# Second attention's scores made by rows in 32-wide column tiles, its maximum subtracted from PSUM, and slot products in column tiles

## The chip, the cores and the metric

The kernel runs on one core of one Trainium2 chip, in fp32 throughout. The metric is device microseconds of one launch. A profile is one execution taken by the hardware profiler; its span is the time from the first to the last instruction.

## The reference

Two stages follow each other: an attention through 32 inducing points for each of 4 batches, and a mixture of 8 experts with 4 slots each, over all 45,824 tokens.

```python
def mab(q, kv):                       # softmax attention, keys are the values
    s = scale * (q @ kv.transpose(0, 2, 1))
    s = s - s.max(-1, keepdims=True)
    a = np.exp(s)
    a /= a.sum(-1, keepdims=True) + 1e-09
    return a @ kv
h = mab(I, x)                         # x: 4 x 11456 x 128, I: 32 x 128 ("first attention")
y = mab(x, h)                         # ("second attention"), y is never stored
logits = y @ phi                      # 45824 x 32 slots
d = softmax of logits over all tokens # per slot
slot_input = d.T @ y                  # 32 x 128
slot_out[e] = relu(slot_input[e] @ w1[e]) @ w2[e]
c = softmax of logits over the 32 slots
out = c @ slot_out                    # 45824 x 128
```

The outputs need `slot_out`, which needs the logits of every token: nothing can be written before the whole input has passed through both attentions.

## The kernel before

**Tiling.** The tokens of a batch are cut into 6 chunks, five of 16 blocks and one of 10 (a block is 128 tokens: four groups of 32). There are 24 chunks n (batch n // 6), and 8 segments of 3 chunks. The matrices of scores have 32 values for each token. They are held in one of two layouts, both 128 partitions by 512 (or 320) columns: "columns", with 4 groups x 32 inducing points or slots on partitions and tokens along the free axis, and "rows", with 128 tokens on partitions and 16 x 32 values along the free axis. A change of layout is a transpose of 32 x 32 pieces by DVE, or one of 128 x 128 pieces by PE into PSUM with a copy by ACT (`pe_turn`).

**Group A** (`group_a`, first attention): load x (`xn`, natural, and for the chunks in HOST_T also `xt`, transposed; for the others PE transposes), scores in columns (`col_mm`, L475), a running maximum over the tokens (DVE L394), exp (ACT), a transpose to rows (`e1`; DVE L420, or PE and ACT for the chunks in TA), the sum over tokens `ha` (PE L426), and POOL's running sum `hz`.

**Group fin** (`group_fin`): from `hz` the batch's h, its transpose `hts` and h @ phi in four copies (`bdg`).

**Group B** (`group_b`, second attention): scores by `col_mm` with `hts` (tile `s2p`, PSUM); then `soft`: transpose to rows (DVE L523), maximum (DVE L527), subtraction (POOL L531), exp (ACT L534), the sum (DVE alone, or after POOL has added halves or quarters: BHALF, BQ), reciprocal, and product (POOL L605), which gives a2, the attention's weights by rows. It is transposed back (L610; PE and ACT for the chunks in TB), multiplied by `bdg` (L613): these are the logits (`lp`), kept in `l_all` for all tokens, with a maximum over the tokens (L618, or L627 for LFUSE).

**Group seg** (`group_seg`), for each segment of three chunks: the maximum (`bch`), exp of the logits (`dt`, L688), its transpose to rows (`d`, L694; TB: PE and ACT), and the slot product `u` = a2^T d (PE L705) over blocks of 128 columns: of the 128 x 128 result only four 32 x 32 blocks on the diagonal are wanted. They are cut out by a mask (`mask_bd`; ACT and POOL, or DVE L719 for the last segment) and multiplied by h (`sip`), which gives `si_all`.

**Group mlp** (`group_mlp`): the segments are joined with weights `wsel`, which carry the normalization (L795), into the slot inputs (L801); then the two layers and `srs`, the slot outputs.

**Groups c and o**: the same `soft` for the output's softmax over slots, in place on `l_all` (TC: the first transpose by PE and ACT), with a transpose back (L909); then `po` = c @ slot_out (PE L926), evicted by ACT or DVE (L937; OD and OD2 name DVE's share), and written by SP's queue.

**Order.** Every step is an `op` of a plan with an engine, a cost and a priority (chunk x SLOPE + LAG of its step). The plan's list scheduler runs them in its own model of time with these costs, with the rings of buffers (RINGS: for instance 7 `xt`, 4 `xn`, 4 `mm` banks of PSUM, of which `s2p` may hold 3), and the instructions are issued in the order that it finds. Groups c mostly fill gaps after A and B; all DMA loads and stores are on SP's queue, and a load into a ring's buffer waits for the last reader of what it held.

Of the kernel before, what the change touches and what calls it, by code (L numbers as in the profile page):

```python
# [15 lines left out]
S = 32  # L16
# [15 lines left out]
TA = [7, 10, 14, 22]  # L32
TB = [14, 15, 18, 19]
# [28 lines left out]

def valid(n):
# [20 lines left out]
SLOPE = {"A": 0.574, "B": 0.622, "c": 0.566, "o": 2.276}  # L84
# [161 lines left out]
def tile_kernel(ctx, tc, xn, xt_d, ind_t, phi, w1, w2, consts, out):  # L246
# [37 lines left out]
    def blocks(t):  # L284
        return t.rearrange("p (j s) -> p j s", s=S)
# [22 lines left out]
    mask_bd = const.tile([P, P], F32, name="mask_bd")  # L308
    nc.vector.tensor_copy(blocks(mask_bd), mask4s)
# [31 lines left out]
    def group_a(a):  # L341
# [120 lines left out]
        op("PE", 0.075 * nb, pr("a2"), a2, [("e1", a), ("xn", a)], [("ha", a)], [("ha", ("ha", a))])  # L462
# [51 lines left out]
    def soft(pre, n, tag, src_keys, src, prio, dst_key, mul, half, turn=False):  # L514
# [6 lines left out]

        def ts():
            nc.vector.transpose(wtile(tag, k("t"))[:, :w], src())  # L523

        def mx():
            m = stile(pre + "m", k("m"), JM)
            nc.vector.tensor_reduce(m[:, :nb], blocks(T[k("t")][:, :w]), axis=AX.X, op=ALU.max)  # L527

        def sb():
            tv = blocks(T[k("t")][:, :w])  # L530
            nc.gpsimd.tensor_tensor(tv, tv, T[k("m")][:, :nb].unsqueeze(2).broadcast_to(full), op=ALU.subtract)  # L531

        def xp():
            nc.scalar.activation(T[k("t")][:, :w], T[k("t")][:, :w], AF.Exp)  # L534
# [30 lines left out]
        if turn:  # L565
            pe_turn(src_keys[0], src, n, tag, k("t"), prio("bts"), virt=("cv",))
# [14 lines left out]
        op("Pool", pl, prio("bml"), ml, [k("z"), k("t")], dst_key[0], dst_key[1])  # L581

# [3 lines left out]
    def group_b(n):  # L586
# [6 lines left out]

        def b1():
            col_mm(ptile("mm", ("s2p", n)), T["hts", b], n)
# [5 lines left out]
        op("PE", 0.9 * z + 0.03, pr("b1"), b1, [("hts", b), ("xt", n)], [("s2p", n)], [("mm", ("s2p", n)), ("s2p", ("s2p", n))])  # L601
# [5 lines left out]
        soft("b", n, "s2", [("s2p", n)], lambda: T["s2p", n][:, :w], pr, ([("a2", n)], [("a2", ("a2", n))]), mul, (n in BHALF) + (n in BQ))  # L607
# [49 lines left out]
    def group_seg(k):  # L657
# [25 lines left out]
        for i, n in enumerate(ns):  # L683
# [12 lines left out]
            def c2(n=n, i=i):  # L696
                if i == 0:
                    ptile("u", ("u", k))
                u, a2, d, w = T["u", k], a2_of(n), T["d", n], width(n)
                offs = list(range(0, w, P))  # L700
                if w % P and i + 1 == SEG:
                    offs = [*offs[:-2], offs[-1], offs[-2]]
                for o in offs:
                    m = min(P, w - o)
                    nc.tensor.matmul(  # L705
                        u[:m, :m], a2[:, o : o + m], d[:, o : o + m],
                        start=i == 0 and o == offs[0], stop=i == SEG - 1 and o == offs[-1],
                    )
# [7 lines left out]
            op("PE", 0.87 * w / 480, pr("c2"), c2, [("d", n), ("a2", n)], [("u", k)], [("u", ("u", k))] if i == 0 else [])  # L716

        def u0():
            nc.vector.tensor_tensor(stile("um", ("um", k), P, 2), T["u", k][:, :P], mask_bd, op=ALU.mult)  # L719

        def u1():
            nc.scalar.copy(stile("us", ("us", k), P, 1), T["u", k][:, :P])

        def u2():
            nc.gpsimd.tensor_tensor(stile("um", ("um", k), P, 2), T["us", k], mask_bd, op=ALU.mult)

        def u3():
            nc.tensor.matmul(ptile("mm", ("sip", k))[:, :P], T["um", k], T["h", b], start=True, stop=True)
# [318 lines left out]
```

## Time and profile before

| what | value |
|---|---|
| median of 3 runs (lowest, highest) | 241.55 us (240.05, 243.39) |
| the profiled execution: time, span | 241.55 us, 239.8 us |
| mean granted TensorE clock | 0.927 |
| PE, DVE, ACT, POOL busy | 84%, 77%, 61%, 62% |
| read, written | 48.81 MB, 23.59 MB |
| first write issued | 178.0 us |

Busy time is the union of an engine's records. PE records are modelled and include the time that a matmul takes through the array. In a group's line the number after the bar is the busy time of all its records, then the mean nanoseconds of one, then the engine's idle time just before them with what ended it. A chain follows the work back from the last instruction to what released each step.

### The profile page before, as it was taken

The page shows a single profiled execution, that of the slowest core. Times are in us where ns is not written, and L with a number is a line of the kernel's source. Part 1 is how long each engine was busy: PE and PEld are TensorE (multiplying, and loading weights), DVE is VectorE, ACT ScalarE, POOL GpSimd, SP SyncE. Part 2 cuts the span into 40 slices and gives each one's busy share as a digit, 9 for nine tenths or more (in the row PEclk, how much of TensorE's full clock was granted, in tenths as well). Part 3 has the DMA queues.
Part 4 walks back from the last instruction along what each step waited for, and adds up shares of the span by engine and source line. Part 5 has one row for each costly group of instructions (what it writes and reads, how often), then busy time and mean ns, then how long its engine had stood idle before and what let it go on. Part 6 is the DMA issues. An engine that isn't in the chain of part 4 may idle for free.

```text
span 239.8 us, 5623 instructions
## 1 busy us (share of the span) xinstructions
PE 201.4 (84%) x2054; PEld 122.8 (51%) x2054; DVE 183.6 (77%) x427; ACT 147.0 (61%) x390; POOL 147.6 (62%) x237
## 2 busy tenths in 40 slices
PE   8899899699999799989999979989977968446370
PEld 8575574336655464637754654776843633211030
DVE  1125529879999699998969989994798999889650
ACT  2687594657747484586737652932259999285460
POOL 0001324979539697097961899986768887777810
PEclk9999999999999999999999999997999799575566
DMA  7999995999999969399996910000019999999977
GB/s 238 415 426 413 391 361 194 413 421 390 340 331 396 418 234 395 101 428 349 399 415 234 425 57 1 0 5 0 3 63 388 395 424 417 416 413 413 423 293 300
DMA packets 13851, 72.76 MB, mean 303 GB/s; under 512 B 1792, under 2 KB 2432, under 8 KB 6912
## 3 DMA queue, kind: packets, MB, share of 16 engines
q1 hardware_dynamic: 13392, 72.23, 76.6%
q8 instruction: 16, 0.26, 0.4%
q10 hardware_dynamic: 432, 0.18, 0.3%
q14 instruction: 11, 0.09, 0.1%
HBM read 48.81 MB, written 23.59 MB: 302 GB/s over the span
## 4 chain that ended last, share of the span: by engine, by line
PE 46%; DVE 15%; ACT 12%; DMA 10%; POOL 9%; issue 5%; ACTq 0%; POOLq 0%; SPq 0%
PE s L475 8%; DMA l_all<-xt 7%; PE po L926 7%; ACT ot L937 6%; PE ha L426 6%; PE lp L613 5%; PE tp L373 4%; PE s2p L475 4%; PE u L705 3%; DMA xt<-xt 3%; PE hpm L825 2%; ACT ct L534 2%; DVE l_all L909 2%; PE warm L317 2%; POOL ct L901 2%
## 5 line engine op out<-in xcount | busy, mean ns | idle before, releaser
L926 PE MATMUL po<-l_all,mb 32*128 32x512 f32 (+1 forms) x192 | 37.6, 783 | 16.1 <-DVE l_all L909 13.2
L937 ACT COPY ot<-po 128x512 f32<-128x512 f32 (+1 forms) x71 | 34.8, 594 | 16.8 <-PE po L926 16.4
L531 POOL TENSOR_TENSOR bt<-bt,bm 128x512 f32<-128x512 f32 (+1 forms) x24 | 23.7, 994 | 20.5 <-DVE bm L527 20.1
L926 PEld LDWEIGHTS po<-l_all,mb 32*128 32x128 f32 x192 | 17.2, 236 | 34.9 <-issue 13.6
L531 POOL TENSOR_TENSOR ct<-ct,cm 128x512 f32<-128x512 f32 (+1 forms) x24 | 23.8, 993 | 11.5 <-DVE cm L527 7.1
L705 PE MATMUL u<-d,a 128*128 128x128 f32 (+1 forms) x184 | 25.4, 281 | 0.4 <-DVE d L694 0.4
L901 POOL TENSOR_TENSOR ct<-ct,cz 128x512 f32<-128x512 f32 (+1 forms) x24 | 23.8, 1001 | 2.7 <-DVE cz L558 2.4
L705 PEld LDWEIGHTS u<-d,a 128*128 128x128 f32 (+1 forms) x184 | 22.3, 189 | 4.9 <-issue 1.0
L605 POOL TENSOR_TENSOR a<-bt,bz 128x512 f32<-128x512 f32 (+1 forms) x24 | 23.9, 995 | 1.5 <-DVE bz L558 1.2
L613 PE MATMUL lp<-a2t,bdg 128*128 128x512 f32 (+1 forms) x48 | 24.0, 594 | 0.9 <-ACT a2t L336 0.6
L394 DVE TENSOR_REDUCE m<-s 128x1 f32<-128x512 f32 (+1 forms) x24 | 15.3, 639 | 11.9 <-PE s L475 11.7
L426 PEld LDWEIGHTS ha<-xn,e 128*32 128x32 f32 x668 | 18.5, 110 | 9.0 <-issue 6.2
L426 PE MATMUL ha<-xn,e 128*32 128x128 f32 x668 | 22.8, 274 | 0.0
L436 POOL TENSOR_TENSOR hz<-hz,al 128x129 f32<-128x129 f32 x20 | 8.0, 398 | 23.2 <-ACT al L433 22.4
L475 PE MATMUL s<-xt,it_sb 128*32 128x512 f32 (+1 forms) x152 | 19.2, 577 | 2.4 <-DMA xt<-xt 1.2
L534 ACT ACTIVATE ct<-ct 128x512 f32<-128x512 f32 (+1 forms) x24 | 15.0, 629 | 9.5 <-POOL ct L531 9.5
L534 ACT ACTIVATE bt<-bt 128x512 f32<-128x512 f32 (+1 forms) x24 | 14.4, 600 | 10.3 <-POOL bt L531 10.1
L909 DVE STREAM_TRANSPOSE l_all<-ct 128x512 f32<-128x512 f32 (+1 forms) x24 | 16.0, 668 | 4.1 <-POOL ct L901 4.1
L937 DVE COPY ot<-po 128x512 f32<-128x512 f32 (+1 forms) x25 | 16.0, 645 | 3.5 <-PE po L926 3.4
L415 ACT ACTIVATE et<-s,negm 128x512 f32<-128x512 f32 (+1 forms) x24 | 15.7, 656 | 4.7 <-DVE negm L410 3.9
L688 ACT ACTIVATE dt<-l_all,negm_l 128x512 f32<-128x512 f32 (+1 forms) x24 | 16.5, 687 | 3.2 <-DVE negm_l L677 2.9
L475 PE MATMUL s2p<-xt,hts 128*32 128x512 f32 (+1 forms) x152 | 17.6, 573 | 0.0
(174 smaller groups left out, 428.2 us busy)
## 6 DMA issues: line engine op xcount, KB each, us to landing
xn<-xn SPq DMA_DIRECT2D x18, 1024.0 KB, 7.1
out<-ot SPq DMA_DIRECT2D x13, 1024.0 KB, 8.6
xt<-xt SPq DMA_DIRECT2D x11, 1024.0 KB, 8.7
w<-w SPq DMA_DIRECT2D x8, 1024.0 KB, 7.5
out<-ot SPq DMA_DIRECT2D x16, 256.0 KB, 2.8
l_all<-xt SPq DMA_DIRECT2D x3, 1024.0 KB, 8.2
out<-ot SPq DMA_DIRECT2D x6, 512.0 KB, 4.1
xt<-xt SPq DMA_DIRECT2D x3, 640.0 KB, 6.0
```

The costliest lines, as they stand in the source:

```text
L426: nc.tensor.matmul(ha[32 * q : 32 * q + 32, :P], T["e1", a][:, j * S : (j + 1) * S], T["xn", a][:, j * P : (j + 1) * P], start=j < 4, stop ...
L475: nc.tensor.matmul(dst[32 * g : 32 * g + 32, :w], lhs, src, start=True, stop=True)
L531: nc.gpsimd.tensor_tensor(tv, tv, T[k("m")][:, :nb].unsqueeze(2).broadcast_to(full), op=ALU.subtract)
L534: nc.scalar.activation(T[k("t")][:, :w], T[k("t")][:, :w], AF.Exp)
L605: nc.gpsimd.tensor_tensor(blocks(a2), blocks(t), zb, op=ALU.mult)
L613: nc.tensor.matmul(ptile("mm", ("lp", n))[:, :w], T["bdg", b], T["a2t", n][:, :w], start=True, stop=True)
L688: nc.scalar.activation(dt_[:, :v], l_of(n)[:, :v], AF.Exp, bias=negm_l[:, k : k + 1], accum_out=z_l[:, k, i : i + 1])
L705: nc.tensor.matmul(u[:m, :m], a2[:, o : o + m], d[:, o : o + m], start=i == 0 and o == offs[0], stop=i == SEG - 1 and o == offs[-1],)
L901: nc.gpsimd.tensor_tensor(blocks(t), blocks(t), zb, op=ALU.mult)
L909: nc.vector.transpose(l_of(n), T["ct", n][:, :w])
L926: nc.tensor.matmul(T["po", 4 * n + g][:, :w], T["srs",][q, :], l_of(n)[q, :], start=True, stop=True)
L937: (nc.vector.tensor_copy if dve else nc.scalar.copy)(ot[:, g * w : (g + 1) * w], T["po", m][:, :w])
```

## The change

1. **Scores by rows** (`group_b`, `b1`): for the chunks in BV, BE and BP, x's transposed blocks of 32 tokens are the weights and `hts` (32 columns) passes through; four column tiles give the 128 tokens of a block. `s2p` is then in rows already.
2. **Modes of `soft`**: T is as before. E copies the rows from PSUM by ACT, and goes on as T. V takes maximum and difference on DVE, straight from PSUM. P takes the negated maximum on DVE from PSUM, adds it into PSUM by a matmul with the identity ("fold"), and ACT's exp reads PSUM. In group c the modes V, E and P (CV, CE, CP, full chunks alone) take their rows from a PE transpose; chunks in CB are turned back by PE and ACT.
3. **Slot products in column tiles** (`c2`): each block of 32 columns is a matmul of its own into one of four column tiles, so `u` is 128 x 32, no mask is needed, and `si_all` has 32 partitions.
4. The normalization leaves `wsel` and goes to `srs`.
5. The lists of chunks (TA, TB, LFUSE, halves, DVE's evictions), and every value of LAG and SLOPE are set anew, so the order of instructions is another.

```diff
-TA = [7, 10, 14, 22]
-TB = [14, 15, 18, 19]
+TA = [1, 4, 7, 10, 14]
+TB = [2, 4, 7, 9, 14, 18, 19]
...
-BHALF = [2, 4, 9, 13, 15, 23]
-CHALF = [2, 3, 6, 11, 12, 15, 17, 21, 23]
-BQ = [0, 5, 7, 9, 14, 18, 23]
-CQ = [0, 4, 9, 10, 12, 15, 18, 20, 22]
-LFUSE = [4, 11, 13, 14, 15, 17, 18, 19, 20, 21, 22, 23]
-OD = [0, 1, 4, 12, 13, 17, 20, 22]
-OD2 = [2, 3, 5, 6, 7, 8, 9, 10, 12, 14, 15, 16, 18, 19, 20, 21, 23]
+BHALF = [2, 4, 9, 13, 15, 17, 18, 19, 23]
+CHALF = [1, 2, 3, 6, 11, 12, 15, 17, 23]
+BQ = [0, 3, 4, 5, 7, 9, 14, 18, 23]
+CQ = [0, 1, 4, 9, 10, 15, 18, 20, 21, 22]
+LFUSE = [4, 10, 11, 13, 14, 15, 17, 18, 19, 20, 21, 23]
+OD = [0, 1, 4, 5, 7, 11, 12, 13, 16, 17, 19, 22]
+OD2 = [2, 6, 8, 10, 15, 18, 20, 21, 23]
...
-TC = [1, 3, 6, 7, 9, 10, 15]
+BV = [1, 3, 6, 9, 15, 18, 21]
+BE = [0, 3, 4, 10, 11, 13, 16]
+BP = [5, 8, 10, 14, 15, 17, 20, 23]
+CV = [3, 5, 6, 9, 10, 17, 19, 23]
+CE = [7, 10, 11]
+CP = [15]
+CB = [0, 8, 17]
...
-SLOPE = {"A": 0.574, "B": 0.622, "c": 0.566, "o": 2.276}
+SLOPE = {"A": 0.454, "B": 0.554, "c": 0.655, "o": 2.411}
...
+        def sv():
+            nc.vector.tensor_tensor(blocks(make()), blocks(src()), mb(), op=ALU.subtract)
+
+        def fold():
+            nc.tensor.matmul(src(), ident, mb(), start=False, stop=True, skip_group_check=True)
...
+        if mode == "T":
+            op("DVE", dv, prio("bts"), ts, [src_key], [k("t")], al)
+        elif mode == "E":
+            op("ACT", ae, prio("bts"), cp, [src_key], [k("t")], al)
+        if mode in "TE":
+            op("DVE", dv, prio("bmx"), mx(tile, False), [k("t")], [k("m")])
+            op("Pool", pl, prio("bsb"), sb, [k("m")], [k("t")])
+            op("ACT", 0.092 + w / 1200, prio("bxp"), xp, [], [k("t")])
+        elif mode == "V":
+            op("DVE", dv, prio("bmx"), mx(src, False), [src_key], [k("m")])
+            op("DVE", dv, prio("bsb"), sv, [src_key, k("m")], [k("t")], al)
+            op("ACT", 0.092 + w / 1200, prio("bxp"), xp, [], [k("t")])
         else:
-            op("DVE", dv, prio("bts"), ts, src_keys, [k("t")], [(tag, k("t"))])
-        op("DVE", dv, prio("bmx"), mx, [k("t")], [k("m")])
-        op("Pool", pl, prio("bsb"), sb, [k("m")], [k("t")])
-        op("ACT", 0.092 + w / 1200, prio("bxp"), xp, [], [k("t")])
+            op("DVE", dv, prio("bmx"), mx(src, True), [src_key], [k("m")])
+            op("PE", 0.03 + 0.86 * w / 512, prio("bsb"), fold, [k("m")], [src_key])
+            op("ACT", 0.092 + w / 1200, prio("bxp"), xs, [src_key], [k("t")], al)
...
+    def mode_of(n, *lists):
+        return next((m for m, x in zip("VEP", lists) if n in x), "T")
...
         def b1():
-            col_mm(ptile("mm", ("s2p", n)), T["hts", b], n)
+            sp = ptile("mm", ("s2p", n))
+            if mode == "T":
+                col_mm(sp, T["hts", b], n)
+                return
+            xt, nb = T["xt", n], SIZES[n % NCH]
+            for j in range(nb):
+                for g in range(4):
+                    o = g * nb * S + j * S if n in TA or n in HOST_T else j * P + g * S
+                    nc.tensor.matmul(
+                        sp[32 * g : 32 * g + 32, j * S : j * S + S], xt[:, o : o + S], T["hts", b],
+                        start=j == 0, stop=True, skip_group_check=True,
+                    )
...
-                for o in offs:
-                    m = min(P, w - o)
-                    nc.tensor.matmul(
-                        u[:m, :m], a2[:, o : o + m], d[:, o : o + m],
-                        start=i == 0 and o == offs[0], stop=i == SEG - 1 and o == offs[-1],
-                    )
+                u, a2, d, nb = T["u", k], a2_of(n), T["d", n], SIZES[n % NCH]
+                for j in range(nb):
+                    q = slice(32 * (j % 4), 32 * (j % 4) + 32)
+                    c = slice(j * S, j * S + S)
+                    nc.tensor.matmul(u[q, :S], a2[:, c], d[:, c], start=i == 0 and j < 4, stop=i == SEG - 1 and j >= nb - 4)
...
-        def g6c():
-            nc.vector.tensor_scalar_mul(T["wsel",], T["wsel",], T["rz", "l"])
...
-            nc.vector.tensor_copy(T["srs",], T["sr",][:, :P])
+            nc.vector.tensor_scalar_mul(T["srs",], T["sr",][:, :P], T["rz", "l"])
...
+            def turn():
+                wtile("cs", ("ct", n))
+                pt = ptile("mm", ("cp", n))
+                for q in range(4):
+                    o = slice(q * P, q * P + P)
+                    nc.tensor.matmul(pt[:, o], l_of(n)[:, o], ident, is_transpose=True, start=q == 0, stop=True, skip_group_check=True)
...
+        if n in CB and whole(n):
+            plan.op("PE", 0.44, pr("bta"), back, [("ct", n)], [("cq", n)], [("mm", ("cq", n)), ("cv", ("cq", n))])
+            plan.touch["ct", n].add(len(plan.ops) - 1)
+            plan.op("ACT", 0.48, pr("bta"), bev, [("cq", n)], [("l", n)])
```

More of the change, by code (lines that the diff above doesn't have):

```diff
@@ L520, in soft, with make, cp, mx @@
         full = (P, nb, S)
+        def make():
+            return T[k("t")][:, :w] if virt else wtile(tag, k("t"))[:, :w]
         def ts():
[L523 to L527, printed above, removed]
-        def sb():
-            tv = blocks(T[k("t")][:, :w])
-            nc.gpsimd.tensor_tensor(tv, tv, T[k("m")][:, :nb].unsqueeze(2).broadcast_to(full), op=ALU.subtract)
+            nc.vector.transpose(make(), src())
+        def cp():
+            nc.scalar.copy(make(), src())
+        def mx(of, neg):
+            def f():
+                m = stile(pre + "m", k("m"), JM)
+                nc.vector.tensor_reduce(m[:, :nb], blocks(of()), axis=AX.X, op=ALU.max, negate=neg)
+            return f
+        def tile():
+            return T[k("t")][:, :w]
+        def mb():
+            return T[k("m")][:, :nb].unsqueeze(2).broadcast_to(full)
+        def sb():
+            tv = blocks(tile())
+            nc.gpsimd.tensor_tensor(tv, tv, mb(), op=ALU.subtract)
+        def sv():
+            nc.vector.tensor_tensor(blocks(make()), blocks(src()), mb(), op=ALU.subtract)
+        def fold():
+            nc.tensor.matmul(src(), ident, mb(), start=False, stop=True, skip_group_check=True)
         def xp():
-            nc.scalar.activation(T[k("t")][:, :w], T[k("t")][:, :w], AF.Exp)
+            nc.scalar.activation(tile(), tile(), AF.Exp)
+        def xs():
+            nc.scalar.activation(make(), src(), AF.Exp)
         def hf():
@@ L600, in group_b @@
         dv = 0.07 + w / 960
-        op("PE", 0.9 * z + 0.03, pr("b1"), b1, [("hts", b), ("xt", n)], [("s2p", n)], [("mm", ("s2p", n)), ("s2p", ("s2p", n))])
+        op("PE", 0.9 * z + 0.03 if mode == "T" else 1.02 * w / 512, pr("b1"), b1, [("hts", b), ("xt", n)], [("s2p", n)], [("mm", ("s2p", n)), ("s2p", ("s2p", n))])
         def mul(t, zb):
@@ L800, in f @@
                 for t in ts:
-                    nc.tensor.matmul(sit[:, :S], si_all[:, t, :], T["wsel",][:, t * S : (t + 1) * S], start=t == 0, stop=t == NSEG - 1)
+                    nc.tensor.matmul(sit[:, :S], si_all[:S, t, :], T["wsel",][:S, t * S : (t + 1) * S], start=t == 0, stop=t == NSEG - 1)
             return f
@@ L878, in group_mlp @@
         op("DVE", 0.07, pr, g6b, [], [("rz",)])
-        op("DVE", 0.26, pr, g6c, [("rz",)], [("wsel",)])
         op("PE", 0.07 * (NSEG - 1), pr, g7(range(NSEG - 1)), [("wsel",), ("mb",)] + [("si", k) for k in ks[:-1]], [("sit",)], [("ha", ("sit",))])
@@ L901, in mul, with back, bev @@
             nc.gpsimd.tensor_tensor(blocks(t), blocks(t), zb, op=ALU.mult)
-        soft("c", n, "cs", [("l", n)], lambda: l_of(n), pr, ([("ct", n)], []), mul, (n in CHALF) + (n in CQ), n in TC)
+        w = width(n)
+        mode = mode_of(n, CV, CE, CP) if whole(n) else "T"
+        if mode == "T":
+            soft("c", n, "cs", mode, lambda: l_of(n), ("l", n), pr, ([("ct", n)], []), mul, (n in CHALF) + (n in CQ))
+        else:
+            def turn():
[4 more added lines that the diff above has]
+                    nc.tensor.matmul(pt[:, o], l_of(n)[:, o], ident, is_transpose=True, start=q == 0, stop=True, skip_group_check=True)
+            plan.op("PE", 0.44, pr("bts"), turn, [("l", n)], [("cp", n)], [("mm", ("cp", n)), ("cv", ("cp", n)), ("cs", ("ct", n))])
+            soft("c", n, "cs", mode, lambda: T["cp", n], ("cp", n), pr, ([("ct", n)], []), mul, (n in CHALF) + (n in CQ), True)
         plan.touch["ct", n].add(len(plan.ops) - 1)
-        w = width(n)
         def t2():
             nc.vector.transpose(l_of(n), T["ct", n][:, :w])
-        plan.op("DVE", 0.07 + w / 960, pr("bta"), t2, [("ct", n)], [("l", n)])
-        plan.touch["ct", n].add(len(plan.ops) - 1)
+        def back():
+            pt = ptile("mm", ("cq", n))
+            for q in range(4):
+                o = slice(q * P, q * P + P)
+                nc.tensor.transpose(pt[:, o], T["ct", n][:, o], ident)
+        def bev():
+            nc.scalar.copy(l_of(n), T["cq", n])
+        if n in CB and whole(n):
+            plan.op("PE", 0.44, pr("bta"), back, [("ct", n)], [("cq", n)], [("mm", ("cq", n)), ("cv", ("cq", n))])
+            plan.touch["ct", n].add(len(plan.ops) - 1)
+            plan.op("ACT", 0.48, pr("bta"), bev, [("cq", n)], [("l", n)])
+        else:
+            plan.op("DVE", 0.07 + w / 960, pr("bta"), t2, [("ct", n)], [("l", n)])
+            plan.touch["ct", n].add(len(plan.ops) - 1)
     def group_o(n):
@@ L1036 @@
         t = res[b, :, j0 * P : (j0 + nb) * P]
-        if (n in TB) ^ (n in TC):
+        if (n in TB) ^ ((n in CV + CE + CP) and whole(n)) ^ (n in CB and whole(n)):
             t = t.reshape(C, 4, nb // 4, 4, 32).transpose(3, 4, 2, 1, 0)
```

53 lines of the change are left out of this document (21 added, 32 removed), and 3 rows, old and new, of the table RINGS.

## The prediction

> **What bounds the kernel now.** I read the page first (shares and slices), then busy time by stage, then the chain of work in order of time, then SP's queue.
>
> ```profile
> span 239.8 us, 5623 instructions
> PE 201.4 (84%) x2054; PEld 122.8 (51%) x2054; DVE 183.6 (77%) x427; ACT 147.0 (61%) x390; POOL 147.6 (62%) x237
> DMA  7999995999999969399996910000019999999977
> HBM read 48.81 MB, written 23.59 MB: 302 GB/s over the span
> ```
>
> A slice is 6 us. DMA is full while x is read, empty in slices 25 to 29, full again while the output is written. The empty stretch is the end of the second attention and the expert network: no output can leave before all logits have been reduced over the tokens. So the time is (end of the last logits) + (expert network) + (writing).
>
> ```profile
> core 0: us, PE busy (x) PEld busy (x) DVE busy (x) ACT busy (x) POOL busy (x), PEclk, DMA share, GB/s
> 36.00:117.00 81.00, 75.07 (x941) 43.13 (x940) 73.81 (x174) 50.72 (x160) 56.46 (x94) 1.00 0.89 340
> 117.00:158.00 41.00, 38.56 (x293) 25.70 (x292) 36.47 (x97) 24.42 (x67) 31.94 (x53) 1.00 0.49 197
> 158.00:178.00 20.00, 17.93 (x259) 12.54 (x258) 14.77 (x35) 6.20 (x13) 14.28 (x21) 0.91 0.01 2
> 178.00:232.00 54.00, 36.50 (x187) 17.32 (x184) 46.59 (x96) 39.27 (x82) 40.36 (x58) 0.75 0.97 392
> ...
> 107.35 3.06 SPq L353 DMA_DIRECT2D xn<-xn  x2
> 178.02 59.06 SPq L944 DMA_DIRECT2D out<-ot  x42
> xn<-xn SPq DMA_DIRECT2D x18, 1024.0 KB, 7.1
> ```
>
> (After the dots: two lines of SP's queue, with start, length and issues; then the median time of such a load to landing.) Until 158 us DVE is busy 91% (73.81 of 81) and 89%; PE 93% and 94%, but PE records contain their own pipeline time, so its figure says less. The last x load is issued near 110 us and lands 7.1 us later, at 117. From 36 to 117 us DMA is 89% busy: 0.11 x 81 = 9 us is all that this stretch can lose while it reads the same bytes. From 178 us writing runs at a share of 0.97; 23.59 MB at that row's 392 GB/s is 60 us of the 61.8 that are left. That stretch is nearly a constant: an earlier first write gives an earlier end, one for one.
>
> ```profile
> 36.16 3.62 PE s2p L475 x32
> 39.82 8.25 DMA l_all<-xt
> 66.77 3.57 PE s2p L475 x32
> 70.40 9.10 DMA l_all<-xt
> 100.86 7.10 DMA xt<-xt
> 130.47 1.20 DVE bt L523 x2
> 139.05 1.01 POOL bt L531
> 159.63 1.16 DVE mb L795
> 160.83 1.97 PE sit L801 x16
> ```
>
> The chain (start, length, what) shows a batch's rhythm: its second scores (s2p) free x buffers, a load follows, then the next batch's first attention. After 123 us it runs over DVE and POOL, through the softmax of the last batch (`bt`), and from 159 us through DVE's scaling of `wsel` (`mb`) and the slot sums.
>
> **The change part by part.** Of 24 chunks of the second attention the lists make 7 V, 6 E, 6 P and 5 T.
>
> *Scores by rows, 19 chunks.* 4 matmuls of 512 columns become 64 of 32 columns. A matmul has two records, so 128 loads and 128 matmuls stand where 8 and 8 were.
>
> ```profile
> 36.09 0.16 PEld L475 LDWEIGHTS s2p<-xt,hts 128*32 128x32 f32 x8 [0.17 <-ACT hts L494]
> L475 PEld LDWEIGHTS s2p<-xt,hts 128*32 128x32 f32 x152 | 4.0, 109 | 6.3 <-issue 4.5 <-DVE mx L618 0.3 <-ACT m L402 0.3
> 63.52 0.99 PE s L475 x8
> 81.47 0.87 PE ha L426 x32
> L801 PE MATMUL sit<-mb,si_all 128*128 128x32 f32 x16 | 2.0, 277 | 0.7 <-DVE mb L795 0.7
> 65.77 1.00 PE u L705 x8
> ```
>
> Eight 32-wide loads take 0.16 us, one 109 ns: they start (160 - 109) / 7 = 7.3 ns apart. So four column tiles accept a load and a matmul every 7 ns. The time goes with the columns that pass: 8 records of 512 take 0.99 us (124 ns each), 32 records of 128 take 0.87 (27 ns). One tile must also reload its weights: 16 records with 128-wide loads and 32 moving columns take (1.97 - 0.28) / 15 = 113 ns each, 0.88 ns a weight column, so 28 ns for 32 columns, 7 ns with four tiles side by side. Both ways give about 7.3 ns: 128 x 7.3 = 0.93 us and some 0.1 to start, what a chunk costs now. The bounds: 0.93 below; above, the 27 ns of the 128-wide records if time does not shrink with width, 128 x 27 = 3.5 us. I take 1.0, because two rows give it on their own, and count nothing.
>
> [...]
>
> *Slot products in 32-wide tiles.* 8 records with 128-wide weights take 1.00 us (65.77); 32 narrow records at 7.3 ns take 0.23, with the start 0.35: -0.65 for 20 chunks, -0.45 for the four short ones, -15 us of PE (bounds: -17, and -3 at 27 ns a record). POOL's masks go.
>
> *DVE and POOL up to 158 us.*
>
> ```profile
> L523 DVE STREAM_TRANSPOSE bt<-s2p 128x512 f32<-128x512 f32 (+1 forms) x24 | 15.6, 662 | 0.7 <-PE s2p L475 0.7
> L531 POOL TENSOR_TENSOR bt<-bt,bm 128x512 f32<-128x512 f32 (+1 forms) x24 | 23.7, 994 | 20.5 <-DVE bm L527 20.1
> L725 POOL TENSOR_TENSOR um<-us,mask_bd 128x128 f32<-128x128 f32 x7 | 3.2, 460 | 0.3
> 56.47 0.44 PE tt_('e1', 10)_859 L333 x4
> L336 ACT COPY e<-tt_('e1', 10)_859 128x512 f32<-128x512 f32 x1 | 0.6, 592 | 0.0
> L613 PE MATMUL lp<-a2t,bdg 128*128 128x512 f32 (+1 forms) x48 | 24.0, 594 | 0.9 <-ACT a2t L336 0.6 <-DVE negm_l L677 0.2
> ```
>
> Two transposes follow each other in 1.20 us (130.47), so one costs 0.60, 0.42 for a short chunk. V puts a subtraction where the transpose was: nothing. E and P drop it: 8 x 0.60 + 4 x 0.42 = 6.5 us. TB grows by three chunks, two transposes each: 3.6. TA grows by one: 0.6. More sums halved by POOL: about 1. DVE loses 11.7 us, of which some 10 belong to chunks before the last batch. POOL loses 13 subtractions (10 x 0.99 + 3 x 0.7 = 12) and 3.2 of masks, and gains about 3 in halvings: -12.
>
> These go to PE and ACT. PE: six folds of 512 or 320 columns as in L613 (two records, 1.0 us, 0.65 when short), 5 us, and seven turns of 0.44, 3 us; with the slot products PE still loses 7. ACT: 13 copies of 0.59, +7.5 us in a stretch where it is busy 63% (50.72 of 81): hidden; without that cover they would cost those 7.5.
>
> The waits added: an s2p bank (three, out of four shared `mm` banks) is held for two DVE operations in V, and for DVE, PE and ACT in P, 0.6 + 1.0 + 0.6 against 0.6 now. Behind a fold stand all of PE's instructions, behind a missing bank the next scores and so SP's x loads. Bounds: nothing, and 1.5 us for each of about 9 V and P chunks before the last batch, 14. I take nothing apart, since DVE, which read those banks, has the more room; the other end is rival 2.
>
> *How much arrives.* Up to 117 us DVE gets 10 of 74 us lighter, but only 9 can be lost before loads bind. I take -6 (bounds 0 and -9). After 117 us the chain is the last batch's softmax: of six chunks four lose POOL's subtraction (3.7 us), two DVE's transpose (1.0), and less is queued from before: -4 (bounds -1 and -8). In the expert network DVE's scaling (1.16 on the chain) goes to 128 columns at the end, and the slot sums for seven segments need no longer wait for it: their 14 records of 113 ns can start near 158.7, when `wsel` is there, and the last two end by about 160.6, against 162.8 now. -2 (bounds -1.2 and -2.5).
>
> *The writing stretch.* The order of the softmax for the outputs is changed wholesale (new LAG, SLOPE), five of its chunks subtract on DVE, one by a fold, two return through PE and ACT, and four evictions move from DVE to ACT.
>
> ```profile
> 178.00:239.80 61.80, 10.61 (x16) 0.74 0.95 382
> ```
>
> That is the last transpose of the output softmax (L909) in that stretch, with its busy time and count: 16 of 24 chunks come after the first write, so this work runs beside the writes. Both engines' sums move by 3 us or less in a stretch where neither is full over the whole (DVE 46.59 and ACT 39.27 of 54). I take 0 (bounds +3, and -3 for the last eight microseconds, where DMA falls off).
>
> Sum on the profiled span: 239.8 - 6 - 4 - 2 = 227.8. That execution took 241.55 us, 1.75 more than its span, and is also the median of the three: 229.5.
>
> **The rivals.** *1. Narrow matmuls are dear* (slower). For it: no row shows a stream of them. Against it: 7.3 ns. At 27 ns, 19 chunks have 280 blocks x 4 x 2 = 2240 records, 60 us against 18 now; the 720 slot records 19 against 23; folds and turns +8: PE +46. PE has 8.4 us of idle by the two rows to 158, so up to 38 stay; part of PE's record time is pipeline, so 30 is likelier: 241.5 + 30 - 2, about 270. It decides from (18 + 23 - 8 + 8 + 12) / 2960 = 18 ns a record, where PE has eaten its idle time and what DVE gave. A second way into the same place:
>
> ```profile
> q8 instruction: 16, 0.26, 0.4%
> ```
>
> PE's instructions come in 16 packets for 4108 recorded instructions, 257 each, 0.4% x 16 x 239.8 / 16 = 1.0 us a packet. A chunk's scores are one such packet, run in 1.0 us: if fetching does not run ahead, 19 chunks pay up to 1 us each, 19. [...] Chance 0.12.
>
> *2. The gain is hidden* (no change). The loads, not DVE, set the pace, since banks and x buffers are freed no earlier and P and V hold s2p longer; what is freed on DVE and POOL is filled with output softmax, which then ends no earlier because of the writes. For it: the loads of 7 to 9 us in the chain. Against it: DVE's 91%. Then only the expert network gains 2 and the last batch 1: 238.5. With held banks it reaches 243. Chance 0.17.
>
> *3. All bounds met.* -9 - 8 - 2.5 - 3: span 217.3, time 219. It needs loads without a gap. Chance 0.05.
>
> **How the numbers follow.** Forecast 229.5, chance 0.66, by itself 222 to 236.5. The three runs lie 1.4% apart, so about 2% is what can be told from no change: under 236.7 is faster. Forecast and rival 3 give faster 0.71; rival 2 same 0.17; rival 1 slower 0.12. The range leaves out rival 1, rival 3 and little else: 219.5 to 242.
>
> **What would show it.** Right: 128 records of `s2p` within about 1.0 us and 32 of `u` in 0.35; DVE's total near 168 and POOL's near 130; last x landing near 111 us, first write near 166, then 61 to 62 us of writes. Wrong: a score chunk over 2 us on PE; PE idle ascribed to banks held by `bm`; x loads that land at 117 as before; or a writing stretch well over 62 us because the output softmax falls behind (DMA share under 0.9).

## The result: a fifth slower, and the profile after

The changed kernel takes 290.87 us (288.97 to 295.14) beside 241.82 for the kernel before: a ratio of 1.200 [1.188, 1.213]. The forecast was 229.5. The profiled execution took 295.14 us and a second one 293.58, both longer than this kernel's other runs; the stalls lie at the same places in both. A ratio compares the undisturbed ("fast") runs alone, with its 95% interval behind it, while a median is over all runs of a kernel, so the two can differ a little.

The page of the changed kernel: span, busy time, granted clock and DMA by slices of 7.3 us, the queue that brings PE's instructions, the shares of the chain.

```profile
span 293.4 us, 11001 instructions
PE 233.4 (80%) x4746; PEld 141.3 (48%) x4746; DVE 172.8 (59%) x404; ACT 154.6 (53%) x404; POOL 130.2 (44%) x217
PEclk9999979789985959995799998999689997565557
DMA  7999838597884646965099783000001999985996
q8 instruction: 37, 0.61, 0.8%
PE 66%; issue 14%; DVE 7%; ACT 4%; POOL 4%; DMA 2%; SPq 0%; ACTq 0%; DVEq 0%; POOLq 0%
```

DVE and POOL have become as light as forecast (172.8 and 130.2 us; 168 and 130 were expected). But DMA, which before was at 9 in all but three of the slices 1 to 20 (slices are counted from 0), has holes down to 3 and 4, PE's instructions fill 37 packets where they filled 16, and 14% of the chain is "issue": PE stands still and waits for nothing that the profile shows. The same stages as before (columns: length, then busy time and count of PE, PEld, DVE, ACT, POOL, granted clock, DMA share, GB/s), and SP's queue:

```profile
36.00:117.00 81.00, 63.72 (x1884) 40.81 (x1887) 45.70 (x103) 38.38 (x113) 35.04 (x60) 0.83 0.66 236
117.00:158.00 41.00, 31.04 (x951) 19.91 (x944) 24.71 (x64) 20.21 (x60) 19.79 (x34) 0.88 0.69 254
...
145.49 2.16 SPq L360 DMA_DIRECT2D xn<-xn  x2
225.16 65.49 SPq L1011 DMA_DIRECT2D out<-ot  x42
```

Every engine is less busy in the same 81 us than before (PE 63.7 for 75.1, DVE 45.7 for 73.8): less gets done per microsecond. The last x load leaves SP at 145.5 to 147.7 us instead of 110, the first write at 225.2 instead of 178.0 (+47), and the writes take 65.5 us instead of 59.1 (+6). PE's timeline, its waits (engine, tile, line, releaser: total us, times, longest) and steps of the chain show where it stands:

```profile
37.81 1.10 PE L651 MATMUL s2p<-hts,xt 128*32 128x32 f32 x104
...
41.61 0.81 PE L651 MATMUL s2p<-hts,xt 128*32 128x32 f32 x43 [2.69 <-issue]
```

```profile
PEld s2p L651 <- issue: 21.1, 18, 5.0
PE s2p L651 <- issue: 17.1, 9, 4.9
PEld ha L433 <- issue: 14.2, 13, 4.4
```

```profile
38.91 2.69 issue
51.38 3.98 issue
99.57 4.08 issue
130.41 4.91 issue
```

A burst of scores runs nearly as fast as forecast: 104 records in 1.10 us, (1.10 - 0.2) / 103 = 8.7 ns apart (7.3 was the estimate; one record takes 0.2). Behind the stop they lie some 14 ns apart (43 in 0.81 us), and why is not shown. Between the two PE stops in the middle of a chunk, with its weights and its bank at hand. These stops are not spread about: with PE's loads and matmuls counted through the trace in order of start, and a gap taken from one start to the next, all eight gaps of 2.5 us and more ahead of the writes fall just behind the same place in a block of 256 recorded instructions (number 193), and the gaps over 0.4 us at this place add up to 37.3 us (43.1 in the second profile). In the records of the queue the packet that goes with the first such stop starts at 39.30 us, 1.7 us after the block before was entered, and lands at 40.26; PE goes on at 41.61.

### The profile page after: what moved, and what is told of

Same layout as the page of the kernel before. It is cut to its first block, busy times and chain, and to the rows that moved or that the text cites. A ratio compares the mean times of both kernels' runs of the same rounds, so it can differ in the third digit from the quotient of the medians.

```text
span 293.4 us, 11001 instructions
## 1 busy us (share of the span) xinstructions
PE 233.4 (80%) x4746; PEld 141.3 (48%) x4746; DVE 172.8 (59%) x404; ACT 154.6 (53%) x404; POOL 130.2 (44%) x217
## 4 chain that ended last, share of the span: by engine, by line
PE 66%; issue 14%; DVE 7%; ACT 4%; POOL 4%; DMA 2%; SPq 0%; ACTq 0%; DVEq 0%; POOLq 0%
PE s L482 9%; PE po L993 9%; PE s2p L651 8%; PE ha L433 8%; PE lp L672 6%; PE tp L380 4%; PE u L763 3%; ACT ot L1004 3%; PE s2p L482 2%; POOL ct L554 2%; PE s2p L560 2%; PE hpm L867 2%; DMA xn<-xn 2%; PE pm L414 2%; PE warm L324 1%
## 5 line engine op out<-in xcount | busy, mean ns | idle before, releaser
L993 PE MATMUL po<-l_all,mb 32*128 32x512 f32 (+1 forms) x192 | 44.1, 820 | 14.8 <-DVE l_all L962 6.3
L1004 ACT COPY ot<-po 128x512 f32<-128x512 f32 (+1 forms) x75 | 37.0, 583 | 17.0 <-PE po L993 14.8
L993 PEld LDWEIGHTS po<-l_all,mb 32*128 32x128 f32 x192 | 16.4, 246 | 38.8 <-ACT ot L1004 25.6
L433 PE MATMUL ha<-xn,e 128*32 128x128 f32 x668 | 26.3, 291 | 9.4 <-issue 9.4
L651 PE MATMUL s2p<-hts,xt 128*32 128x32 f32 x1648 | 18.5, 201 | 9.4 <-issue 9.4
L482 PE MATMUL s<-xt,it_sb 128*32 128x512 f32 (+1 forms) x152 | 22.1, 626 | 3.4 <-issue 2.6
L651 PEld LDWEIGHTS s2p<-hts,xt 128*32 128x32 f32 x1648 | 16.8, 111 | 14.7 <-issue 11.5
L554 POOL TENSOR_TENSOR ct<-ct,cm 128x512 f32<-128x512 f32 (+1 forms) x18 | 17.6, 978 | 10.8 <-DVE cm L543 10.0
L543 DVE TENSOR_REDUCE bm<-s2p 128x16 f32<-128x512 f32 (+1 forms) x13 | 8.4, 643 | 20.9 <-PE s2p L651 20.7
L554 POOL TENSOR_TENSOR bt<-bt,bm 128x512 f32<-128x512 f32 (+1 forms) x11 | 11.2, 1020 | 21.2 <-DVE bm L543 21.1
L451 POOL TENSOR_TENSOR hz<-hz,hs 128x129 f32<-128x129 f32 x20 | 9.2, 462 | 22.4 <-ACT hs L448 22.4
L571 POOL TENSOR_TENSOR ch<-ct 128x256 f32<-128x256 f32 (+1 forms) x17 | 11.8, 697 | 15.0 <-ACT ct L563 10.0
```

The costliest lines, as they stand in the source:

```text
L433: nc.tensor.matmul(ha[32 * q : 32 * q + 32, :P], T["e1", a][:, j * S : (j + 1) * S], T["xn", a][:, j * P : (j + 1) * P], start=j < 4, stop ...
L482: nc.tensor.matmul(dst[32 * g : 32 * g + 32, :w], lhs, src, start=True, stop=True)
L554: nc.gpsimd.tensor_tensor(tv, tv, mb(), op=ALU.subtract)
L651: nc.tensor.matmul(sp[32 * g : 32 * g + 32, j * S : j * S + S], xt[:, o : o + S], T["hts", b], start=j == 0, stop=True, skip_group_check=True,
L993: nc.tensor.matmul(T["po", 4 * n + g][:, :w], T["srs",][q, :], l_of(n)[q, :], start=True, stop=True)
L1004: (nc.vector.tensor_copy if dve else nc.scalar.copy)(ot[:, g * w : (g + 1) * w], T["po", m][:, :w])
```

## The experiments

**Theory F (fetch):** PE's instructions arrive in blocks of 256; about one block is there ahead, a new one takes some 4 us, and the scores consume one in 1.0 us. **Rival A (array):** narrow matmuls cost array or decode time that their records don't show. **Rival O (order):** the new order and lists cost the time. The expectations below call A "theory R" and O "theory H".

### Is it the number of instructions?

*e2_before_dummy*: the kernel before with its own order and its wide scores, and 60 (or 36) idle 32-wide matmuls ahead of them in 19 chunks. *e3_before_twice*: the same, but the wide scores twice: the same array time with 16 instructions instead of 240. *e1_after_wide*: the changed kernel with BV, BE and BP empty, all scores wide, its own order. *e9_after_free*: the changed kernel with its order, lists and modes to the instruction, but the score matmuls wide, so that the softmax runs over the other axis.

```diff
# e2
+ for i in range(4 * SIZES[n % NCH] - 4):
+     g = 32 * (i % 4)
+     nc.tensor.matmul(sp[g : g + 32, :S], T["xt", n][:, g : g + S], T["hts", b], start=True, stop=True)
  col_mm(sp, T["hts", b], n)
# e3
+ col_mm(sp, T["hts", b], n)
  col_mm(sp, T["hts", b], n)
# e1
- BV, BE, BP = [1, 3, 6, ...], [0, 3, 4, ...], [5, 8, 10, ...]
+ BV, BE, BP = [], [], []
# e9, in b1
- if mode == "T":
+ if True:
      col_mm(sp, T["hts", b], n)
```

> The changed kernel with the second attention's scores made in columns for all chunks again, so mode T everywhere in group b; narrow slot products, lists, LAG and SLOPE stay. Theory F (PE's instructions come in blocks of 256, one block ahead, about 4 us each, and a chunk's 64 narrow score matmuls are 256 instructions that run in 1 us): some 4200 PE instructions fewer, no waits of PE at block boundaries, 232 to 246 us. Theory H (the new order and the held PSUM banks lost the time): 270 us or more stays, since order and lists stay. Theory R (narrow matmuls are dear in the array): as F.

> The kernel before, same order, with 60 idle narrow matmuls (36 in a short chunk) of the same form ahead of the wide scores in the 19 chunks that the change makes by rows; their result is overwritten. That adds 240 PE instructions and 0.95 us of array time to each. F: three to four us a chunk where PE has no slack, 275 to 300 us. R: array time alone, 0.95 us x 19 = 18 us at most, 242 to 260 us. H: nothing beyond array time, as R.

> The kernel before, with the wide scores of the same 19 chunks made twice into the same bank: 16 PE instructions and 1.0 us of array time more in each, so the same array time as the run with idle narrow matmuls without its instructions. F: well under that run, 243 to 260 us. R and H: the same time as that run within 2%.

> The changed kernel with its order of steps, its lists and all its modes kept to the letter; only the instructions of a chunk's scores differ: 4 wide matmuls, which leave them in columns, where the 64 narrow ones stood (so the softmax runs over the wrong axis, on the same shapes). It leaves out what makes the layout. F: all stops at block boundaries go, and what is left is the change as the prediction's sum took it, with scores at 1.0 us and few instructions: by that sum 229.5 us, 222 to 238. H (the order and the held banks have a price of their own): 245 us or more.

| kernel | median us | ratio [95%] | instruction packets | first write, us |
|---|---|---|---|---|
| e2, 240 idle instructions a chunk | 283.76 | 1.172 [1.162, 1.182] | 32 | 220.2 |
| e3, 16 instructions of equal array time | 250.58 | 1.034 [1.025, 1.044] | 17 | 186.9 |
| e1, changed, scores wide in mode T | 254.80 | 1.050 [1.042, 1.059] | 21 | 185.4 |
| e9, changed, scores wide, order kept | 245.45 | 1.003 [0.995, 1.010] | 21 | 175.9 |

The waits of e2:

```profile
PEld s2p L600 <- issue: 24.3, 29, 4.2
PE s2p L600 <- issue: 18.6, 12, 4.1
```

In the old order, idle narrow matmuls make the same stop at the same tile, and the gaps at the block's edge add up to 27.0 us. So O does not explain the loss. Of e2's 41 us (242.4 was measured beside it for the kernel before), 33 (283.8 - 250.6) go with the 240 narrow instructions and not with the array time that their records show. A price that each narrow matmul has beside its record is not excluded by e2 and e3, since e3's matmuls are wide; the place of the gaps in the block speaks against it, and e5, below, decides it. e9 closes the account from the other side: with everything of the change but the form of the scores' instructions the ratio falls from 1.200 to 1.003. So nearly all of the loss, 45 of the 49 us by the medians, goes with the scores' instructions; what e9 lacks beside the forecast is another matter, below. e1 lies above the 232 to 246 us that F gave. Its gaps at block edges are gone (1.5 us in all), but with all modes T the plan makes an order of its own, with a later first write (185.4 us) and writes that take 66.2 us.

### What a block costs

*e5_burst*: before, with the warm-up replaced by 4 x 256 matmuls of 32, 64, 128 and 32 columns in four column tiles, which wait for nothing.

```diff
- warm(("warm0",), WARM)
+ for cols in (32, 64, 128, 32):
+     for i in range(256):
+         g = 32 * (i % 4)
+         nc.tensor.matmul(T["warm0",][g : g + 32, :cols], wz[:, g : g + 32], wz[:, :cols], start=True, stop=True)
```

> The kernel before, its 8 matmuls of warming at the start replaced by 1024 that wait for nothing: 256 each of 32, 64, 128 and again 32 moving columns, in four column tiles, all of one weight width; 16 blocks of 256 PE instructions. Theory F (instructions come at one block in about 4 us): all four parts take about the same, 13 to 17 us, with stops at block boundaries, and the narrow records between the stops lie 8 ns apart. Theory R (array time): 4, 7, 14 and 4 us. The kernel's own time only shifts by the length of the burst.

The run took 302.85 us; the kernel itself follows about 60 us later than without the burst. PE's timeline of e5 (start, length, records of a block's matmuls, idle time before):

```profile
1.03 3.21 PE L958 MATMUL warm<-wz 128*32 128x32 f32 x223 [1.03 <-DVE wz L313]
7.94 1.93 PE L958 MATMUL warm<-wz 128*32 128x32 f32 x128 [3.69 <-issue]
14.14 1.94 PE L958 MATMUL warm<-wz 128*32 128x32 f32 x128 [4.26 <-issue]
20.33 2.96 PE L958 MATMUL warm<-wz 128*32 128x32 f32 x128 [4.26 <-issue]
...
27.52 1.99 PE L958 MATMUL warm<-wz 128*32 128x64 f32 x128 [1.74 <-issue]
31.24 1.99 PE L958 MATMUL warm<-wz 128*32 128x64 f32 x128 [1.74 <-issue]
...
38.43 12.60 PE L958 MATMUL warm<-wz 128*32 128x128 f32 x512 [0.46 <-issue]
52.52 1.28 PE L958 MATMUL warm<-wz 128*32 128x32 f32 x128 [1.49 <-issue]
56.52 1.69 PE L958 MATMUL warm<-wz 128*32 128x32 f32 x128 [2.72 <-issue]
60.25 1.93 PE L958 MATMUL warm<-wz 128*32 128x32 f32 x128 [2.03 <-issue]
```

The stages of e5 with the x loads (DMA share 0.98) and without (0.02):

```profile
14.00:20.00 6.00, 1.94 (x128) 1.80 (x128) 0.00 (x0) 0.00 (x0) 0.00 (x0) 1.00 0.98 408
26.00:34.00 8.00, 3.98 (x256) 3.67 (x256) 0.00 (x0) 0.00 (x0) 0.00 (x0) 1.00 0.02 4
```

The first stop comes after some 450 records (223 matmuls and as many loads). After that each stretch is x128: 128 weight loads and 128 matmuls, one packet. While the first x loads run, blocks start 6.2 us apart (7.94, 14.14, 20.33); later 3.7 us (27.52 to 31.24, 56.52 to 60.25), for 32 columns and for 64. The row of x512 holds four blocks, of which the last 95 matmuls have 32 columns again and all others 128. They start 3.5 to 3.7 us apart as well (at 38.43, 41.88, 45.61 and 49.06, the next at 52.52), but here the matmuls themselves fill that time. The width changes inside a block, at 20.79, 35.17 and 50.00 us, so the four parts take 19.8, 14.4, 14.8 and 14.3 us: F had 13 to 17 for each, which the first, beside the loads, exceeds; A had 4, 7, 14 and 4. So the price goes by the block and not by the columns, and A falls: 3.73 / 128 = 29 ns for a load and its matmul with the DMA engines quiet, 48 ns beside the loads. Inside a block records lie 8.5 to 14 ns apart (128 in 1.28 and in 1.93 us); 8 were expected. An estimate from this for the changed kernel: from 36 to 117 us it got through (1884 + 1887) / 256 = 14.7 blocks, 55 us of fetching by 3.73 and 91 by 6.2, in a stretch of 81.

### Three ways round it

*e6_after_64*: rows in two 64-wide column tiles, half the instructions. *e7_after_spread*: each chunk's narrow scores as four plan steps, with other PE work between them. *e11_lists_last*: the kernel's old lists and order, rows in 64-wide tiles for chunks 18, 20, 21 and 23 alone, where the loads are over; beside it *e10_lists_wide*, the same without any rows.

```diff
# e6
- for g in range(4): ... sp[32 * g : 32 * g + 32, ...], xt[:, o : o + S]
+ for g in range(2): ... sp[64 * g : 64 * g + 64, ...], xt[:, o : o + 64]
# e7
+ for part in range(4):
+     op("PE", 0.9 * w / 512, pr("b1"), lambda part=part: b1(part), ...)
# e11 (e10: all three empty), old TA, TB, LAG, SLOPE, halves and evictions
+ BV, BE, BP = [], [], [18, 20, 21, 23]
```

> The changed kernel with the scores by rows in two column tiles of 64 tokens: 32 matmuls a chunk in place of 64, 128 instructions in place of 256, plan cost 1.85 us in place of 1.02; for that x's transposed blocks lie one after the other in all chunks. Modes, narrow slot products, lists, LAG and SLOPE stay. F: 64 records at about 28 ns, 1.8 us of array time, slow enough for the fetch nearly everywhere: most of the loss goes, 238 to 262 us, PE waits at block boundaries under 10 us. R (what is narrow is dear in the array, 27 ns a record or more): the same per record, half the records, half of the loss goes, 265 us. H (order and held banks): 275 us or more.

> The changed kernel with a chunk's scores by rows as four steps of the plan (16 narrow matmuls, 64 instructions each) at 0.9 us each, which is the pace of the fetch, in place of one at 1.02. The same instructions, but the list scheduler leaves room between and puts other work of PE there. F: stops become shorter, some of the 49 us come back, 255 to 285 us; not all, since 34 blocks at 4 us fill 136 of the first 200 us. R: no gain, 285 us or more.

> The changed kernel's code with every list, LAG and SLOPE of the kernel before and no chunk by rows: narrow slot products and the normalization moved from wsel to the end are all that is left of the change. From the run with narrow slot products in the old order (same as before) less 1.2 us of DVE on the chain and up to 2.5 of the slot sums: 238 to 244 us.

> As the run just named, with four chunks of the last batch (18, 20, 21, 23) by rows in two tiles of 64 tokens and in mode P, where the chain runs over DVE and POOL: DVE loses four transposes (2.2 us), POOL four subtractions (3.7), PE gains four folds and 3.6 us of array time. F: 128 instructions in 1.9 us stay under the fetch's pace, so no stops; 235 to 242 us, a version a little under the kernel before. If PE is the bound in the last batch as well: 242 to 247.

e6: 264.82 us, 1.089 [1.077, 1.102], 28 packets. F had 238 to 262, A 265. The gaps at block edges add up to 5.3 us only, so it is not the stops; the price has moved into the array:

```profile
36.00:117.00 81.00, 77.59 (x1583) 54.05 (x1571) 60.17 (x143) 50.18 (x147) 46.02 (x78) 1.00 0.78 298
```

PE is busy 96% of this stretch, and DMA's share is 0.78 where it was 0.89. The 64-wide scores of the 19 chunks have 36.6 us of PE records, where the wide ones of as many tokens had some 18 (an estimate from the 22.5 us of all 24 chunks before). e7: 282.76 us, 1.165 [1.155, 1.176], block-edge gaps 22.6 us: spreading helps a little (290.9 to 282.8), as it must if the mean rate and not only the bursts is too high. e10: 244.46, 1.005 [1.000, 1.010]. e11: 248.79, 1.023 [1.016, 1.031], its first write 8.9 us later than e10's (186.9 and 178.0). 235 to 242 had been expected of it, or 242 to 247 if PE was the bound in the last batch as well; its order is another too, so which of the two costs the 8.9 us is not told apart. Fewer narrow matmuls cost less; no version with scores by rows came out faster than the kernel before.

### Where the forecast gain went

With the stalls gone, e9 should by the sum have reached about 230. It is at the 245 or more that theory H gave for it: the new order and the modes do not explain the loss, but they may well explain why the gain is missing. Its stages and SP's queue:

```profile
36.00:117.00 81.00, 76.60 (x1164) 40.48 (x1164) 67.70 (x163) 56.26 (x170) 53.22 (x92) 0.98 0.90 340
...
108.81 2.13 SPq L360 DMA_DIRECT2D xn<-xn  x2
175.87 64.57 SPq L1011 DMA_DIRECT2D out<-ot  x42
```

DVE is 6.1 us lighter up to 117 us (67.70 for 73.81), yet the last x load leaves SP when it did before, at 110.9. The first write comes 2.1 us earlier, and the writes take 5.5 us longer (64.6; 65.3 in a second profile, *e18_after_free_again*). Three steps of the sum were then tried alone, in the old order: *e12_dve_light* takes the maxima of chunks 0 to 17 over a quarter of the elements, *e8_before_slot_order* has the slot products in column tiles (*e4_before_slot* the same, with the plan's costs and so the order changed), *e13_load_light* loads half of `xt` for six chunks. *e14_dve_pe_light* is e12 with e8, *e15_all_light* all three.

```diff
# e8, e4 (um, mask_bd and their steps go as in the change)
- nc.tensor.matmul(u[:m, :m], a2[:, o : o + m], d[:, o : o + m], ...)
+ nc.tensor.matmul(u[q, :S], a2[:, c], d[:, c], ...)   # 32-wide blocks, four column tiles
# e12 (and L394 likewise)
- nc.vector.tensor_reduce(m[:, :nb], blocks(T[k("t")][:, :w]), axis=AX.X, op=ALU.max)
+ nc.vector.tensor_reduce(m[:, :nb], tv[:, :, : S // 4] if pre == "b" and n < 18 else tv, axis=AX.X, op=ALU.max)
# e13
- nc.sync.dma_start(xtile("xt", a)[:, :xw], xt_d[HOST_T.index(a)][:, :xw])
+ nc.sync.dma_start(xtile("xt", a)[:, :xh], xt_d[HOST_T.index(a)][:, :xh])
```

> The kernel before with one part of the change alone: slot products as 32-wide matmuls in column tiles, no mask. PE gets about 15 us lighter and issues about 1070 instructions more, spread over 24 places of 64. F: a few of these places meet a block boundary, most don't; -8 to +2 us on the kernel before. R: narrow matmuls dear (27 ns a record) takes most of the gain away, 0 to -3 us. H: as F.

> The kernel before with narrow slot products, every step's cost and place in the order kept as before (the last mask becomes a copy on DVE, the others a step that issues nothing). If the narrow slot products by themselves cost time: 245 us or more, as in the run with their own plan. If it was only the new order that the smaller cost made: 236 to 242 us.

> The kernel before with both maxima (first attention L394, second L527) of chunks 0 to 17 taken over a quarter of the elements, which leaves out three quarters of these 36 reductions; order and all else as before. DVE is 13.5 us lighter before the last batch, with nothing added elsewhere. Theory D (DVE sets the pace up to the last load, as the prediction's sum said): the last x load and the end come 6 to 9 us earlier, 232 to 236 us. Theory L (loads and the buffers that they wait for) or P (PE): 239 to 243 us.

> The kernel before with only half of the transposed x loaded for chunks 11, 12, 13, 14, 16 and 17 (the scores read that half twice; it leaves out the rest): 6.5 us of DMA less between 45 and 107 us, all engines as busy as before. L: the last x load lands 4 to 7 us earlier and the end follows, 234 to 238 us. D or P: 239 to 243 us.

> DVE lighter as in e12 and PE 15 us lighter by the narrow slot products of e8 in one kernel, old order. If DVE and PE hold each other up in turn (either alone gains nothing): 230 to 236 us. L: 239 to 244 us.

> DVE, PE and the loads lighter together (e12, e8, e13). L: as e13 alone or a little better, 232 to 238 us. If the three bound together: 226 to 232 us.

| kernel | median us | ratio [95%] | last x load ends on SP | first write | clock 36-117 |
|---|---|---|---|---|---|
| before | | 1 | 110.4 | 178.0 | 1.00 |
| e12, DVE lighter | 242.27 | 0.998 [0.993, 1.002] | 109.6 | 178.9 | 0.98 |
| e8, PE lighter | 243.87 | 1.006 [1.001, 1.011] | 110.0 | 178.6 | 0.98 |
| e4, PE lighter, own order | 246.38 | 1.016 [1.010, 1.023] | 106.7 | 183.7 | 0.98 |
| e13, loads lighter | 240.28 | 0.989 [0.982, 0.996] | 109.3 | 178.6 | 0.98 |
| e14, e12 + e8 | 247.76 | 1.022 [1.015, 1.030] | 112.9 | 180.8 | 0.94 |
| e15, all three | 240.20 | 0.992 [0.988, 0.997] | 108.0 | 178.8 | 0.94 |

The stages of e12 up to 117 us, then of e14:

```profile
36.00:117.00 81.00, 77.61 (x949) 44.65 (x948) 66.51 (x176) 51.69 (x163) 57.53 (x95) 0.98 0.89 346
```

```profile
36.00:117.00 81.00, 70.46 (x1148) 37.49 (x1142) 62.18 (x167) 48.74 (x154) 52.77 (x87) 0.94 0.88 335
```

e12 takes 7.3 us from DVE in this stretch, more than the change does, and the last load moves by 0.8 us, the time not at all. DVE does not set that pace, though it is busy 91%. Lighter loads gain 1.1% (expected: 234 to 238 us if the loads were the bound), a lighter PE nothing, and DVE and PE together lose 2.2%. In e14 the granted clock is lower too (0.94; over the run 0.872 for 0.927), but e15 has the same 0.94 and 0.870 at 240.20 us, so the lower clock by itself does not explain the loss. From e14 to e15, with DVE and PE light in both, the lighter loads are worth 7.6 us; yet e15 stays above the 226 to 238 that were expected, and e14 above its 230 to 244. What sets the pace up to the last load stays open: in the old order no resource alone had that load earlier by more than 1.1 us (e13), the three together by 2.4, and the first write not at all (the profiled executions of e13 and e15 took 242.1 and 242.3 us, so they show little of the gain). e4, at +4 us where -8 to +2 were expected, has its loads end 3.7 us earlier and its first write 5.7 later: an earlier last load does not bring an earlier end with it, as the sum had it.

### The normalization alone

*e16_before_norm*: the kernel before, its order kept, with the normalization alone moved from `wsel` to the last copy.

```diff
-            nc.vector.tensor_scalar_mul(T["wsel",], T["wsel",], T["rz", "l"])
+            pass
...
-            nc.vector.tensor_copy(T["srs",], T["sr",][:, :P])
+            nc.vector.tensor_scalar_mul(T["srs",], T["sr",][:, :P], T["rz", "l"])
```

> The kernel before, order and costs as they are, with the normalization alone moved from wsel (DVE 1.16 us on the chain) to the last copy of the slot outputs. By the prediction's third term -1.2 us (the slot sums still start together): 240 to 241.5 us, ratio 0.995, at the edge of what five rounds tell. If DVE's next instructions fill the place and the sums wait for si_all: no change.

It takes 240.11 us, 0.987 [0.980, 0.993]: 1.3% under the kernel before, a small difference from four and nine runs. It is the one part of the change that by itself lowered the time. Its PE timeline, SP's queue and the stage around the expert network:

```profile
160.23 1.87 PE L801 MATMUL sit<-mb,si_all 128*128 128x32 f32 x16
...
176.69 59.03 SPq L944 DMA_DIRECT2D out<-ot  x42
```

```profile
158.00:178.00 20.00, 17.58 (x270) 12.99 (x270) 15.28 (x37) 7.47 (x15) 15.19 (x21) 1.00 0.03 11
```

The slot sums start 0.6 us earlier (160.23 for 160.83) and the first write 1.3 us (176.69 for 178.02). The granted clock of this stage was 1.00 where the profile of before has 0.91, so a part of that 1.3 us may be clock.

The second profiles of the changed kernel and of e9, taken to see whether stalls and longer writes repeat, did so (first write 223.6 and writes of 65.4 us in the changed kernel):

> The changed kernel once more for a second profile: 288 to 292 us, waits of PE at block boundaries 30 to 40 us in all, first write near 222 us.

> The kernel e9 once more for a second profile. If the writing stretch is longer in every execution: first write near 176 us, then 64 us or more to the end of SP's issues against 59 before. If that was only the disturbed execution: 60 to 62 us and a time near 240.

## Why the prediction was wrong, by its steps

- **"Count nothing" for the scores' instructions: the step that failed.** The array time was nearly right (104 of a chunk's 128 records in 1.10 us; 1.0 us a chunk was taken), though behind a stop records lie some 14 ns apart. What 256 instructions cost to bring was not in the sum: 3.7 to 6.2 us (e5) for a chunk that the sum lets run in 1.0. In place of nothing it cost some 45 us (the changed kernel less e9).
- **Rival 1's second way was the right one, mis-sized and held unlikely.** It was priced at the packet's own transfer, 1 us each and 19 in all. The transfer measures 0.95 us, but from entering the block before to going on it is 4.0 us (37.6 to 41.6 in the changed kernel). There are 21 packets more, since the slot products and folds add some too. Its chance of 0.12 was for both ways together and was the author's estimate: no view of the kernel before shows how far ahead PE's instructions are fetched. e5 shows about one block: it stops after some 450 recorded instructions and then after each 256. The row of the profile that held the warning, 257 instructions to a packet, stands in the prediction.
- **The first way, 27 ns a record, was wrong.** Inside a burst records lie 8.7 ns apart (104 in 1.10 us), and some 14 behind a stop (43 in 0.81 us), both under the 18 at which it would have decided.
- **-6 up to 117 us: failed in its premise.** DVE's 91% was read as a bound. e12 took 7.3 us from DVE there and got nothing. Rival 2 ("the gain is hidden") describes them better; it gave 238.5 to 243, and e12 measured 242.27, e9 a little more, 245.45.
- **-4 in the last batch and -2 in the expert network: at most -2 of them came.** e9's first write is 2.1 us earlier, and e16 alone gives 1.3. The -4 is not seen.
- **0 in the writing stretch: mis-sized.** With the changed kernel's order it takes 5 to 6 us longer in all four profiles (64.6 and 65.3 in e9, 65.5 and 65.4 in the changed kernel; 59.1 before), beyond the bound of +3. e1 and e6, with the same lists in orders of their own, have 66.2 and 62.3. The lists and modes by themselves do not do it: e7 has them too, in yet another order and with less of the output softmax left for this stretch (POOL 28.1 us for 36.1 in e9), and writes in 57.8. Weight loads of the output matmuls wait longer for ACT's evictions, 25.2 us in e9 where it was 8.3 before. But they wait less for other things: all idle time ahead of them grew from 34.9 to 38.2 us only. The granted clock is lower as well. What leads was not tried. The waits of e9 and of before, then the output matmuls alone in the writing stretch, before (L926) and in e18 (L993):

```profile
PEld po L993 <- ACT ot L1004: 25.2, 22, 4.5
```

```profile
PEld po L926 <- ACT ot L937: 8.3, 15, 3.1
```

```profile
178.00:238.00 60.00, 35.85 (x180) 16.48 (x176) 0.75 0.97 391
```

```profile
178.00:240.00 62.00, 40.49 (x176) 14.81 (x170) 0.67 0.89 358
```

PE's 36 us of them became 40 at a clock of 0.67 instead of 0.75, and DMA's share fell from 0.97 to 0.89.

- **Held:** DVE's and POOL's sums, and the slot products' own price: their PE group went from 25.4 us to 11.2, 14 for the 15 forecast. In e8 that was worth no time.

## What to carry to other kernels

Before a matmul is cut into narrow ones, count the instructions and not only the columns: a row of the profile that gives instructions per packet, and the distance of blocks in a burst, say how many a microsecond PE can be fed (here 256 in 3.7 us, or 6.2 while x loads filled the DMA engines). Here, above that rate, the few wide matmuls cost 33 us less than the many narrow ones of equal array time (e2 and e3). An engine that is 91% busy is a bound only if taking work from it moves the end, and one experiment that makes it lighter tells that before a rewrite does.

## What the runs showed of the hardware that was not expected

- PE's instruction supply has a rate of its own: one block of 256 recorded instructions in 3.5 to 3.7 us, 6.2 us while x loads fill the DMA engines (share 0.98), about one block ahead: the first stop comes after some 450 records (all e5). A packet itself takes some 1.0 us in both stretches of e5. In its records the packet starts 3.6 to 3.8 us after the block before was entered while the loads run, and 1.0 to 1.1 us without them. Whether it is the loads that hold it up was not tried apart.
- In four column tiles a load and a matmul came every 8 to 9 ns in a burst of the changed kernel (104 records in 1.10 us) and in one block of e5 (128 in 1.28), but every 14 ns in e5's first burst (223 in 3.21 us) and in three of its blocks of 32 columns behind a stop (128 in 1.93 or 1.94 us).
- Where PE is less busy between 36 and 117 us, the granted clock tends to be lower there: 1.00 before (PE busy 93%), 0.94 in e14 (87%), 0.83 and 0.89 in the changed kernel's two profiles (79% and 72%). It is a tendency and not a rule: the less busy of these two has the higher clock, e8 has 0.98 at 88%, and e15 has 0.94 at 91%.
